# One row of u spread by a matrix product, the diagonal's fills in halves, and a planner with new durations

## The chip, the cores and the metric

The kernel runs on one core of a Trainium2 chip. The metric is the device time of one execution in microseconds. Five engines work side by side, each through its own instructions in order: TensorE (PE, with its weight loads, PEld, shown apart), VectorE (DVE), ScalarE (ACT), GpSimd (POOL) and SyncE (SP), which here only issues transfers.

## The reference, cut to what matters

A linear attention over 768 positions, 4 batches and 8 heads of width 48, whose output goes, token by token, through a feed-forward layer with a cosine gate:

```python
for t in range(S):                       # (B, H, S, D) = (4, 8, 768, 48)
    cur = einsum('bhd,bhe->bhde', u[None] * k[:, :, t], v[:, :, t])
    y[:, :, t] = einsum('bhd,bhde->bhe', r[:, :, t], state + cur)
    state = w[None, :, :, None] * state + einsum('bhd,bhe->bhde', k[:, :, t], v[:, :, t])
x = y.transpose(0, 2, 1, 3).reshape(3072, 384)
h = x @ w_in                             # (3072, 2048)
out = (h * cos(h)) @ w_out               # (3072, 384)
```

u, of shape (8, 48), weighs only the current position, so it enters on the diagonal of the position by position matrix alone.

## The kernel before, in words

The 3072 tokens are 24 chunks of 128 positions (chunk i is batch i % 4, position block i // 4). The function `chunk` does the attention of one chunk, and these are its steps with their lines in the kernel before:

- SP loads k, r and v of the chunk, 192 KB each, in pieces of 192 bytes (L638 for k and v, L654 for r). There are three buffers for k, three for v and two for r. From chunk 12 on, k and r are loaded a second time in another layout (L659), and r itself goes into one of the eight buffers `f`.
- PE transposes r and k (L696); DVE or ACT takes the result out of PSUM, with the decay factors (L721, L747, L756). From chunk 12 on DVE transposes instead (L704), and POOL applies the decay (L709).
- POOL multiplies r by k (L731), the product by u (L760), and k by its decay `dec_k` (L739). DVE sums L760's result by head (L766, `a`).
- ACT fills the diagonal: for each pair of heads it writes the identity times `a` into a 128x128 block of `A` (L775, eight instructions for each chunk, in two planned operations of four).
- PE computes the position by position products (L785); DVE copies their upper part over the diagonal (L791, needs the fills); PE makes x from the state (L805) and from `A` and v (L818), and the next state (L840). ACT and DVE split x into two parts (L868, L873).

The feed-forward layer runs over blocks of three chunks. A step is one slice f of 128 of the 2048 hidden columns: nine matmuls make h (L282), then ACT (`qi`, L293), DVE (`rest`, L296), ACT (`cos`, L299), DVE (`gate`, L986), ACT (`gh`, L989) and DVE (`gl`, L992) make the gated value in two parts, and nine matmuls (L288) add it to three accumulators. There are 128 such steps. Finished accumulators are copied out by ACT or DVE (L1019, L1021) and stored by SP, or added to the output in memory by POOL (L1034). Weights come as 64-bit numbers, 384 KB a piece (`raw`, L472 and L477, two buffers), and are converted by ACT, DVE and POOL (L556, L564, L576, L587, L592, L597). The buffers `f` are shared by the gates, by the products of L731, by conversion and by outputs.

The order of all this is not written out. Every piece of work is an `op` with an engine, a due time, a planned duration (`cost`), a planned latency (`lat`) until others may use its result, the ops it comes after, and its buffers. A list scheduler (`Plan.order`, L149) places the ops on the engines by these numbers, in five passes and one more, and picks buffers as it goes; the program is emitted in the planned order. Ops that share `line="..."` keep their order among themselves. While the first steps run, PE is kept busy by small matmuls on a tile of zeros ("warm-ups", L1050): one for each 0.2 us for which the plan sees PE idle (L1056 to L1059). So a changed duration anywhere can change the order everywhere.

Before the first chunk, w is loaded (L396), transposed (L401), raised to powers on DVE (L406 to L416) and spread to the decay tables `decT_k` and `decT_r` (L422); `dec_k` is `decT_k` transposed by PE (L438) and copied by ACT (L442). u is loaded by one transfer which reads the same 1536 bytes for each of the 128 partitions (L451).

Of the kernel before, what the change touches and what calls it, by code (L numbers as in the profile page):

```python
# [216 lines left out]
def kernel(  # L217
# [11 lines left out]
    nc = tc.nc  # L229
# [72 lines left out]
    with ExitStack() as actx:  # L302
# [80 lines left out]
        def start_dve():  # L383
            nc.vector.memset(warm, 0.0)
            nc.vector.memset(pq[:, :, 0:1], 1.0)

# [10 lines left out]
            [],  # L397
            lat=2.2,
        )
        b_w = Buf(B_EARLY)  # L400
# [30 lines left out]


        b_tab = Buf(B_EARLY)

# [5 lines left out]
        def tab_copy():  # L440
# [3 lines left out]
        o_tt = op(PE, -6, 0.5, tab_t, [o_dtk, o_pool], [b_tab], lat=0.3)  # L444
        o_dk = op(ACT, -6, 0.45, tab_copy, [o_tt], [b_tab])

        o_u = op(
            SP,
            -23.9,
            1.2,  # L450
            lambda: nc.sync.dma_start(u_b.rearrange("p h d -> p (h d)"), u.rearrange("h d -> (h d)").partition_broadcast(P)),  # L451
            lat=3.0,
        )

# [75 lines left out]
        def conv(i, due, behind=None):  # L530
# [17 lines left out]
            def cn():  # L548
# [13 lines left out]
                due - 2.1,  # L562
                0.33,
                lambda: nc.vector.tensor_scalar(  # L564
# [57 lines left out]
        def chunk(i, due, xbuf):  # L622
# [62 lines left out]
            if late:  # L685
                l_ks = op(SP, due - 6.2, 2.2, load_s(ks, k), ahead, [ks], lat=4.0, line=ln)
                l_rs = op(SP, due - 6.1, 2.2, load_s(rs, r), ahead, [rs], lat=4.0, line=ln)
            l_k = op(SP, due - 5.2, 1.2, load(kb, k), ahead, [kb], lat=2.6, line=ln)
            l_r = op(SP, due - 5.1, 1.2, load_r, ahead, [rb], lat=2.6, line=ln)
# [25 lines left out]
            else:  # L715
                t_r = op(PE, due - 2.4, 0.43, tr(rTp, rb), [l_r, o_pool], [rb, rTp, rT], lat=0.3)
                e_r = op(
# [23 lines left out]
            if first:  # L741
                t_k = op(PE, due - 2.5, 0.43, tr(kTp, kb), [l_k, o_pool], [kb, kTp, kT], lat=0.3)
                e_k = op(
                    DVE,
                    due - 2.3,
                    0.62,
                    lambda: nc.vector.tensor_tensor(kT()[0:KP], cube(kTp)[0:KP], decT_k[0:KP], op=ALU.mult),  # L747
                    [t_k, o_dtk],
                    [kTp, kT],
                )  # L750
                o_kd = op(e2, due + 1.0, c2, decay_k, [t_k, o_m, o_dk], [kb], port=True)
            else:
                o_kd = op(e2, due - 2.7, c2, decay_k, [o_m, o_dk], [kb], port=True)
            if not first and not late:
                t_k = op(PE, due - 2.5, 0.43, tr(kTp, kb), [o_kd, o_pool], [kb, kTp, kT], lat=0.3)
                e_k = op(ACT, due - 2.3, 0.5, lambda: nc.scalar.copy(kT()[0:KP], cube(kTp)[0:KP]), [t_k], [kTp, kT])  # L756
# [13 lines left out]

            def diagonal(j):
                def go():
                    for p in range(NP):
                        h = 2 * p + j
# [3 lines left out]

            o_d = [op(ACT, due - 1.55 + 0.01 * j, 1.18, diagonal(j), [o_a, o_pool], [ab, A[j]], line="diagonal") for j in range(2)]

# [5 lines left out]

            last_A[0] = o_A = op(PE, due - 1.7, 1.3 if late else 1.1, mm_a, [e_k, e_r], [kT, rT, *Ap], lat=0.3)

# [5 lines left out]

            e_A = [op(DVE, due - 1.4 + 0.01 * j, 0.65, mask(j), [o_A, o_d[j], o_pool2], [Ap[j], A[j]]) for j in range(2)]

# [54 lines left out]
            if late:  # L851
# [3 lines left out]
                    due - 0.7,  # L855
                    (0.9 if c else 0.0) + 1.3 + (0.55 if more else 0.0),
                    mm_xz,
# [4 lines left out]
            else:  # L862
                xo1 = None
                if c:
                    xo1 = op(PE, due - 0.7, 0.8, mm_x, [e_r, *e_A, *o_zt], [rT, xp, zb], lat=0.3)
                xo2 = op(PE, due - 0.65, 1.03, mm_x2, [xo1, l_v, o_pool, *e_A], [vb, *A, xp], lat=0.3)

# [334 lines left out]
```

## Time and profile before

| what | us |
|---|---|
| median of 3 runs (lowest, highest) | 518.86 (518.16, 519.00) |
| the profiled execution's own time | 519.36 |
| its span, first to last instruction | 517.6 |
| busy: PE, DVE, ACT, POOL | 505.2, 392.2, 331.7, 176.7 |
| mean granted TensorE clock, share of full speed | 0.995 |

Times in the profile are microseconds from the span's start. "Busy" of PE counts a matmul until its modelled end, so it can show 10 of 10 us although matmuls overlap; an idle gap of PE is a real gap. Warm-ups count as busy. In a row of the waits, "A <- B" says that A sat idle until B ended. The chain of waits follows the work that ended last back to the start.

### The profile page before, as it was taken

How to read it: one execution, taken by the hardware profiler on the slowest of the kernel's cores; microseconds unless marked ns; L12 is line 12 of the kernel's file. 1: busy time of each engine (PE TensorE's matmuls, PEld its weight loads, DVE VectorE, ACT ScalarE, POOL GpSimd, SP SyncE). 2: the span in 40 equal slices, each digit the busy share in tenths (PEclk: the TensorE clock that was granted, in tenths of full speed). 3: DMA queues.
4: the chain of work that ended last, by engine and by line, in shares of the span. 5: the costliest groups of instructions: out<-in, count | busy, mean ns of one | idle time of the engine just before them, and what ended most of it. 6: DMA issues, size and time to landing. Idle time of an engine off the chain costs nothing.

```text
span 517.6 us, 11730 instructions
## 1 busy us (share of the span) xinstructions
PE 505.2 (98%) x4401; PEld 480.6 (93%) x4401; DVE 392.2 (76%) x773; ACT 331.7 (64%) x833; POOL 176.7 (34%) x184
## 2 busy tenths in 40 slices
PE   8999999999999999999999999999999999999994
PEld 5788889999999998999999999999999999999993
DVE  6789988888888887666777887788787767766552
ACT  3889987777677765536566566585665765654452
POOL 6786522354454434232425134134134041300000
PEclk9999999999999999999999999999999999999998
DMA  8988345468556475424585646456536555210001
GB/s 133 174 159 188 72 139 182 146 134 180 137 139 131 114 164 97 78 61 69 144 152 120 150 129 169 89 177 155 132 85 154 170 136 121 80 46 2 2 0 53
DMA packets 114980, 61.61 MB, mean 119 GB/s; under 512 B 78433, under 2 KB 110818, under 8 KB 114914
## 3 DMA queue, kind: packets, MB, share of 16 engines
q1 hardware_dynamic: 109586, 53.50, 41.6%
q0 software_dynamic: 5184, 7.08, 9.2%
q8 instruction: 36, 0.59, 0.5%
q14 instruction: 30, 0.25, 0.2%
q10 hardware_dynamic: 144, 0.20, 0.1%
HBM read 48.96 MB, written 11.80 MB: 117 GB/s over the span
## 4 chain that ended last, share of the span: by engine, by line
PE 90%; DMA 3%; DVE 2%; POOL 1%; ACT 0%; issue 0%; SPq 0%; DVEq 0%; POOLq 0%; ACTq 0%
PE bank L288 38%; PE bank L282 37%; PE bank L785 4%; PE bank L818 4%; PE bank L805 3%; PE bank L696 2%; PE bank L840 2%; DMA raw<-in_moe_w_in_dram 1%; DMA r<-in_r_dram 1%; DMA u_b<-in_u_dram 1%; DVE gl L992 1%; DVE f L296 0%; POOL f L587 0%; POOL k L739 0%; POOL f L760 0%
## 5 line engine op out<-in xcount | busy, mean ns | idle before, releaser
L288 PE MATMUL bank<-w_out_hi,gh 128*128 128x384 f32 x384 | 131.4, 342 | 0.1
L288 PE MATMUL bank<-w_out_hi,gl 128*128 128x384 f32 x384 | 129.8, 338 | 1.3 <-DVE gl L992 1.3
L282 PE MATMUL bank<-xh,w_in_hi 128*128 128x384 f32 x384 | 130.1, 339 | 0.0
L282 PE MATMUL bank<-xh,w_in_lo 128*128 128x384 f32 x384 | 129.5, 337 | 0.0
L288 PE MATMUL bank<-w_out_lo,gh 128*128 128x384 f32 x384 | 129.5, 337 | 0.0
L282 PE MATMUL bank<-xl,w_in_hi 128*128 128x384 f32 x384 | 128.8, 335 | 0.0
L992 DVE TENSOR_TENSOR gl<-f,gh 128x384 fp32r<-128x384 f32 (+1 forms) x132 | 84.4, 642 | 28.2 <-ACT gh L989 27.2
L299 ACT ACTIVATE f<-f 128x384 f32<-128x384 f32 (+1 forms) x132 | 67.3, 513 | 52.7 <-DVE f L296 50.8
L293 ACT ACTIVATE qi<-bank 128x384 int32<-128x384 f32 (+1 forms) x132 | 62.7, 478 | 59.1 <-PE bank L282 58.1
L986 DVE TENSOR_TENSOR f<-bank,f 128x384 f32<-128x384 f32 (+1 forms) x132 | 71.2, 542 | 35.6 <-ACT f L299 32.9
L296 DVE SCALAR_TENSOR_TENSOR f<-bank,qi 128x384 f32<-128x384 f32 (+1 forms) x132 | 71.0, 541 | 34.8 <-ACT qi L293 33.9
L989 ACT CAST gh<-f 128x384 fp32r<-128x384 f32 (+1 forms) x132 | 65.8, 500 | 47.0 <-DVE f L986 41.7
L288 PEld LDWEIGHTS bank<-w_out_hi,gh 128*128 128x128 f32 x384 | 72.0, 187 | 2.7 <-ACT f L1019 0.5
L282 PEld LDWEIGHTS bank<-xh,w_in_hi 128*128 128x128 f32 x384 | 72.1, 188 | 1.7 <-issue 0.2
L288 PEld LDWEIGHTS bank<-w_out_hi,gl 128*128 128x128 f32 x384 | 72.0, 188 | 1.6 <-DVE gl L992 1.6
L282 PEld LDWEIGHTS bank<-xh,w_in_lo 128*128 128x128 f32 x384 | 72.1, 188 | 0.2 <-DVE w_in_lo L597 0.2
L282 PEld LDWEIGHTS bank<-xl,w_in_hi 128*128 128x128 f32 x384 | 72.1, 188 | 0.0
L288 PEld LDWEIGHTS bank<-w_out_lo,gh 128*128 128x128 f32 x384 | 72.0, 187 | 0.0
L775 ACT ACTIVATE A<-ident,a 128x128 f32<-128x128 f32 x192 | 59.9, 390 | 2.3 <-DVE a L766 2.3
L587 POOL TENSOR_TENSOR f<-f,raw 128x384 int32<-128x384 int32 x32 | 36.1, 1129 | 72.5 <-DVE f L576 19.4
L709 POOL TENSOR_TENSOR kT<-kT,decT_k 112x512 f32<-112x512 f32 x12 | 16.4, 1365 | 125.8 <-DVE kT L704 87.4
L1034 POOL DMA_DIRECT2D out_dram<-f x36 | 33.1, 1144 | 32.0 <-ACT f L1019 27.9
(88 smaller groups left out, 601.9 us busy)
## 6 DMA issues: line engine op xcount, KB each, us to landing
raw<-in_moe_w_in_dram SPq DMA_DIRECT2D x32, 384.0 KB, 3.8
raw<-in_moe_w_out_dram SPq DMA_DIRECT2D x32, 384.0 KB, 3.1
out_dram<-f POOLq DMA_DIRECT2D x36, 192.0 KB, 5.3
k<-in_k_dram SPq DMA_DIRECT2D x24, 192.0 KB, 4.1
v<-in_v_dram SPq DMA_DIRECT2D x24, 192.0 KB, 4.7
raw<-in_k_dram SPq DMA_DIRECT2D x47, 96.0 KB, 3.1
raw<-in_r_dram SPq DMA_DIRECT2D x47, 96.0 KB, 2.1
out_dram<-f SPq DMA_DIRECT2D x23, 192.0 KB, 2.3
```

Of the source, the lines that this page charges most:

```text
L282: nc.tensor.matmul(ph, a, b_, start=(i == 0), stop=(i == len(mm) - 1))
L288: nc.tensor.matmul(acc, a[:, ts], b_[:, f, :], start=(first and i == 0), stop=(last and i == 2))
L293: nc.scalar.activation(qi, ph, AF.Copy, scale=INV_2PI, bias=0.25)
L296: nc.vector.scalar_tensor_tensor(q, ph, INV_2PI, qi, op0=ALU.mult, op1=ALU.subtract)
L299: nc.scalar.activation(q, q, AF.Sin, scale=TWO_PI, bias=0.5 * math.pi)
L587: lambda: nc.gpsimd.tensor_tensor(ai(), ai(), cn(), op=ALU.add),
L775: nc.scalar.activation(A[j]()[:, p, :], ident, AF.Copy, scale=ab()[:, h : h + 1])
L785: nc.tensor.matmul(cube(Ap[j])[:, p, :], kT()[ps, p, :], rT()[ps, p, :], start=True, stop=True)
L986: nc.vector.tensor_tensor(g()[:, cs], ph()[:, cs], q()[:, cs], op=ALU.mult)
L989: nc.scalar.copy(gh()[:, cs], g()[:, cs])
L992: nc.vector.tensor_tensor(gl()[:, cs], g()[:, cs], f32(gh())[:, cs], op=ALU.subtract)
L1034: nc.gpsimd.dma_start(dst, ob(), accum_op=ALU.add)
```

## The change

There are four edits.

1. u is loaded as one row of 1536 bytes into partition 0 of its table. PE multiplies a row of 128 ones (kept in the first row of `dec_k` until that is written) by it, which gives u in all 128 partitions in PSUM, and ACT copies it to the table. The write of `dec_k` now also comes after that product.
2. The diagonal's fills, planned as two operations of four instructions (1.18 each), are four operations of two (0.59 each). The instructions are the same.
3. Planned durations are altered: 0.33 to 0.27 for a DVE step of the conversion, 0.43 to 0.49 for PE's transposes, 1.3 to 1.25 for the late chunks' products, 1.03 to 1.06 for x, and the late chunks' combined x and state by 0.25 at most.
4. The load of w and the load of k of the first chunk are put on one line, so they keep their order.

```diff
+            nc.vector.memset(dec_k.rearrange("p h d -> p (h d)")[0:1, 0:P], 1.0)
...
+        u_f, ones = u_b.rearrange("p h d -> p (h d)"), dec_k.rearrange("p h d -> p (h d)")[0:1, 0:P]
+        b_u = Buf(B_EARLY)
+        o_u0 = op(SP, -23.9, 0.1, lambda: nc.sync.dma_start(u_f[0:1], u.rearrange("(o h) d -> o (h d)", o=1)), lat=2.2)
+        o_u1 = op(
+            PE,
+            -20,
+            0.6,
+            lambda: nc.tensor.matmul(b_u()[:, 0:DM], ones, u_f[0:1], start=True, stop=True),
+            [o_u0, o_dve],
+            [b_u],
+            lat=0.3,
+        )
+        o_u = op(ACT, -20, 0.45, lambda: nc.scalar.copy(u_f, b_u()[:, 0:DM]), [o_u1], [b_u])
...
-        o_dk = op(ACT, -6, 0.45, tab_copy, [o_tt], [b_tab])
-
-        o_u = op(
-            SP,
-            -23.9,
-            1.2,
-            lambda: nc.sync.dma_start(u_b.rearrange("p h d -> p (h d)"), u.rearrange("h d -> (h d)").partition_broadcast(P)),
-            lat=3.0,
-        )
+        o_dk = op(ACT, -6, 0.45, tab_copy, [o_tt, o_u1], [b_tab])
...
-                0.33,
+                0.27,
...
-                t_r = op(PE, due - 2.4, 0.43, tr(rTp, rb), [l_r, o_pool], [rb, rTp, rT], lat=0.3)
+                t_r = op(PE, due - 2.4, 0.49, tr(rTp, rb), [l_r, o_pool], [rb, rTp, rT], lat=0.3)
...
-            def diagonal(j):
+            def diagonal(j, ps):
                 def go():
-                    for p in range(NP):
+                    for p in ps:
...
-            o_d = [op(ACT, due - 1.55 + 0.01 * j, 1.18, diagonal(j), [o_a, o_pool], [ab, A[j]], line="diagonal") for j in range(2)]
+            o_d = [
+                [
+                    op(ACT, due - 1.55 + 0.01 * j, 0.59, diagonal(j, ps), [o_a, o_pool], [ab, A[j]], line="diagonal")
+                    for ps in ((0, 1), (2, 3))
+                ]
+                for j in range(2)
+            ]
```

The whole order comes out anew. Three places show it; lines of the kernel after are higher by 1 to 15 (L647 and L663 are the loads of k, v and of r, L481 a piece of w_in, L718 the decay on POOL, L740, L748 and L769 the products by k, `dec_k` and u, L1049 the output's accumulating store). A name's number is its buffer.

The first place is the start of SP's queue, where the loads of w, u and the first chunks stand. Before:

```order
L396 DMA wr<-in_w_dram 4x2x48
L638 DMA k_86<-in_k_dram 128x8x48
L654 DMA r_84<-in_r_dram 128x8x48
L451 DMA u_b<-in_u_dram 128x384
L638 DMA k_87<-in_k_dram 128x8x48
L654 DMA r_85<-in_r_dram 128x8x48
L638 DMA v_89<-in_v_dram 128x8x48
```

After, the same stretch:

```order
L397 DMA wr<-in_w_dram 4x2x48
L437 DMA u_b<-in_u_dram 1x384
L647 DMA k_86<-in_k_dram 128x8x48
L663 DMA r_84<-in_r_dram 128x8x48
L647 DMA v_89<-in_v_dram 128x8x48
L647 DMA k_87<-in_k_dram 128x8x48
L663 DMA r_85<-in_r_dram 128x8x48
```

u has moved ahead of the first k and is one row; v of chunk 0 has moved ahead of k and r of chunk 1.

The second place is SP's queue from r of chunk 2 (the second use of buffer 84) to r of chunk 4 (its third). Before:

```order
L654 DMA r_84<-in_r_dram 128x8x48
L638 DMA v_90<-in_v_dram 128x8x48
L654 DMA r_85<-in_r_dram 128x8x48
L638 DMA k_86<-in_k_dram 128x8x48
L638 DMA v_91<-in_v_dram 128x8x48
L654 DMA r_84<-in_r_dram 128x8x48
```

After:

```order
L663 DMA r_84<-in_r_dram 128x8x48
L647 DMA v_91<-in_v_dram 128x8x48
L663 DMA r_85<-in_r_dram 128x8x48
L647 DMA k_86<-in_k_dram 128x8x48
L481 DMA raw_118<-in_moe_w_in_dram 128x3x256
L647 DMA v_89<-in_v_dram 128x8x48
L647 DMA k_87<-in_k_dram 128x8x48
L663 DMA r_84<-in_r_dram 128x8x48
```

As many loads stand ahead of r of chunk 3 (buffer 85) as before; but between it and r of chunk 4 there are now four transfers, one of them the first piece of w_in, where there were two. On PE, which then transposes r of chunk 4, the plan has put four warm-ups in front of those transposes; before there were none.

The third place is POOL's queue around chunk 12, the first one that POOL itself decays. Before:

```order
L709 TENSOR_TENSOR kT_94<-kT_94,decT_k 112x512
L1034 DMA out_dram<-f_112 128x384
L1034 DMA out_dram<-f_108 128x384
L1034 DMA out_dram<-f_110 128x384
L731 TENSOR_TENSOR f_111<-f_106,k_86 128x384
L709 TENSOR_TENSOR rT_96<-rT_96,decT_r 112x512
L760 TENSOR_TENSOR f_111<-f_111,u_b 128x384
L739 TENSOR_TENSOR k_86<-k_86,dec_k 128x8x48
```

After:

```order
L718 TENSOR_TENSOR kT_94<-kT_94,decT_k 112x512
L740 TENSOR_TENSOR f_108<-f_106,k_86 128x384
L718 TENSOR_TENSOR rT_96<-rT_96,decT_r 112x512
L748 TENSOR_TENSOR k_86<-k_86,dec_k 128x8x48
L769 TENSOR_TENSOR f_108<-f_108,u_b 128x384
L1049 DMA out_dram<-f_105 128x384
L1049 DMA out_dram<-f_107 128x384
L1049 DMA out_dram<-f_106 128x384
```

The three stores of a finished block stood ahead of the chunk's four products and now stand behind them, and the product by u has become the last of the four.

More of the change, by code (lines that the diff above doesn't have):

```diff
@@ L398 @@
             lat=2.2,
+            line="begin",
         )
@@ L687, in chunk @@
                 l_rs = op(SP, due - 6.1, 2.2, load_s(rs, r), ahead, [rs], lat=4.0, line=ln)
-            l_k = op(SP, due - 5.2, 1.2, load(kb, k), ahead, [kb], lat=2.6, line=ln)
+            l_k = op(SP, due - 5.2, 1.2, load(kb, k), ahead, [kb], lat=2.6, line="begin" if i == 0 else ln)
             l_r = op(SP, due - 5.1, 1.2, load_r, ahead, [rb], lat=2.6, line=ln)
@@ L741, in chunk @@
             if first:
-                t_k = op(PE, due - 2.5, 0.43, tr(kTp, kb), [l_k, o_pool], [kb, kTp, kT], lat=0.3)
+                t_k = op(PE, due - 2.5, 0.49, tr(kTp, kb), [l_k, o_pool], [kb, kTp, kT], lat=0.3)
                 e_k = op(
@@ L754, in chunk @@
             if not first and not late:
-                t_k = op(PE, due - 2.5, 0.43, tr(kTp, kb), [o_kd, o_pool], [kb, kTp, kT], lat=0.3)
+                t_k = op(PE, due - 2.5, 0.49, tr(kTp, kb), [o_kd, o_pool], [kb, kTp, kT], lat=0.3)
                 e_k = op(ACT, due - 2.3, 0.5, lambda: nc.scalar.copy(kT()[0:KP], cube(kTp)[0:KP]), [t_k], [kTp, kT])
@@ L785, in mm_a @@
                         nc.tensor.matmul(cube(Ap[j])[:, p, :], kT()[ps, p, :], rT()[ps, p, :], start=True, stop=True)
-            last_A[0] = o_A = op(PE, due - 1.7, 1.3 if late else 1.1, mm_a, [e_k, e_r], [kT, rT, *Ap], lat=0.3)
+            last_A[0] = o_A = op(PE, due - 1.7, 1.25 if late else 1.1, mm_a, [e_k, e_r], [kT, rT, *Ap], lat=0.3)
             def mask(j):
@@ L793, in mask @@
                 )
-            e_A = [op(DVE, due - 1.4 + 0.01 * j, 0.65, mask(j), [o_A, o_d[j], o_pool2], [Ap[j], A[j]]) for j in range(2)]
+            e_A = [op(DVE, due - 1.4 + 0.01 * j, 0.65, mask(j), [o_A, *o_d[j], o_pool2], [Ap[j], A[j]]) for j in range(2)]
             def xv():
@@ L855, in chunk @@
                     due - 0.7,
-                    (0.9 if c else 0.0) + 1.3 + (0.55 if more else 0.0),
+                    (0.8 if c else 0.0) + 1.15 + (0.5 if more else 0.0),
                     mm_xz,
@@ L865, in chunk @@
                     xo1 = op(PE, due - 0.7, 0.8, mm_x, [e_r, *e_A, *o_zt], [rT, xp, zb], lat=0.3)
-                xo2 = op(PE, due - 0.65, 1.03, mm_x2, [xo1, l_v, o_pool, *e_A], [vb, *A, xp], lat=0.3)
+                xo2 = op(PE, due - 0.65, 1.06, mm_x2, [xo1, l_v, o_pool, *e_A], [vb, *A, xp], lat=0.3)
             x_h = op(ACT, due - 0.4, 0.42, lambda: nc.scalar.copy(xbuf()[0], xv()), [xo2], [xp, xbuf])
```

## The prediction

> **What bounds the kernel now.** I read the page's first lines, then the busy time by stretch, then PE's waits, then the chain of waits over the first 72 us.
>
> ```profile
> span 517.6 us, 11730 instructions
> PE 505.2 (98%) x4401; PEld 480.6 (93%) x4401; DVE 392.2 (76%) x773; ACT 331.7 (64%) x833; POOL 176.7 (34%) x184
> ```
>
> ```profile
> 0.00:10.00 10.00, 7.70 (x48) 5.22 (x48) 6.00 (x21) 1.96 (x3) 5.79 (x21) 1.00 0.70 122
> 10.00:20.00 10.00, 8.93 (x154) 7.11 (x153) 7.66 (x14) 7.55 (x24) 8.15 (x9) 1.00 1.21 164
> 20.00:30.00 10.00, 10.00 (x187) 8.21 (x184) 8.06 (x16) 9.39 (x30) 7.45 (x8) 1.00 0.93 175
> 30.00:40.00 10.00, 9.89 (x186) 8.23 (x184) 9.19 (x18) 8.41 (x25) 8.55 (x9) 1.00 0.92 176
> ...
> 150.00:200.00 50.00, 48.75 (x279) 48.43 (x278) 41.69 (x75) 31.51 (x69) 23.41 (x23) 1.00 0.70 147
> 200.00:250.00 50.00, 50.00 (x422) 48.24 (x422) 32.30 (x62) 29.26 (x71) 11.19 (x11) 1.00 0.37 72
> ...
> 500.00:518.00 18.00, 10.07 (x58) 9.75 (x56) 6.03 (x22) 6.08 (x22) 0.00 (x0) 0.86 0.11 39
> ```
>
> The columns after the stretch and its length are the busy time of PE, PEld, DVE, ACT and POOL, then clock, DMA share and GB/s. PE sets the time: after the first 20 us it is idle for 0.11 us in one early stretch, for 1.25 us between 150 and 200, and for 7.93 us at the tail after its last matmul. The clock is full. The matmuls are the same in both kernels but for one, so the change can only move PE's idle time and its warm-ups. Where that idle time comes from is in PE's waits (total us, times, longest):
>
> ```profile
> PE bank L288 <- DVE gl L992: 1.3, 1, 1.3
> PE bank L1050 <- DVE pq L385: 1.1, 1, 1.1
> PE bank L696 <- DMA r<-in_r_dram: 1.1, 2, 0.8
> PE bank L438 <- DVE decT_k L422: 0.7, 1, 0.7
> PE bank L696 <- DMA k<-in_k_dram: 0.5, 2, 0.3
> ```
>
> Four of the five belong to the start; the first is the gap near 197. The chain shows which wait of the start ends last (start, us, what):
>
> ```profile
> 2.83 5.29 DMA u_b<-in_u_dram
> ...
> 8.25 1.31 POOL f L760
> ...
> 10.50 1.01 POOL f L731
> ...
> 11.53 5.47 DMA r<-in_r_dram
> ...
> 17.04 0.65 PE bank L696 x4
> 17.70 0.11 PE bank L1050
> ...
> 20.21 1.09 PE bank L785 x16
> ...
> 21.88 0.49 PE bank L840 x16
> 22.38 0.58 PE bank L696 x4
> ```
>
> u lands at 8.12, POOL's three products follow, the third frees r's buffer for chunk 3, that load lands at 17.00, and PE, which had only warm-ups until then, goes on and has hardly a gap after it. At 22.38 it transposes r of chunk 4 without a wait.
>
> **Part 1: u as one row.** What the old transfer cost its neighbours is seen in three landings on which somebody waited:
>
> ```profile
> 6.07 1.01 POOL L731 TENSOR_TENSOR f<-r,k 128x384 f32<-128x384 f32 x1 [2.27 <-DMA r<-in_r_dram]
> ```
>
> ```profile
> 10.33 0.62 PE L696 MATMUL bank<-ident,r 128*112 128x128 f32 x4 [0.27 <-DMA r<-in_r_dram]
> ...
> 13.85 0.40 PEld L696 LDWEIGHTS bank<-ident,r 128*112 128x112 f32 x4 [0.20 <-DMA r<-in_r_dram]
> ```
>
> r of chunk 0, 1 and 2 are there by 6.07, 10.33 and 13.85. Between the last two lie three ordinary loads (v0, k2, r2): 3.52 us, 1.17 each. Between the first two lie u, k1 and r1: 4.26 us. So u took 4.26 - 2 x 1.17 = 1.92 us of the transfer queue, 0.75 more than an ordinary load. The new row adds an issue ahead of everything; the nearest row is the load of w as one row of the same length near the end:
>
> ```profile
> L459 SPq DMA_DIRECT2D f<-in_w_dram x1: 308/308/308, 463.9 to 463.9; - x1
> ```
>
> That is 0.31 us. An ordinary load stands where u stood, so from r1 on everything in the same place of the queue lands 0.75 - 0.31 = 0.44 us earlier, and r of chunk 3 at 17.00 - 0.44 = 16.56. It can't be held up by its issue: POOL's L731 of chunk 1, at 10.50 before, still waits for r1 (10.33 - 0.44) and for `dec_k`, and two loads are queued between r1's landing and r3's. The product by ones stands behind w's transpose on PE and needs a row issued right behind w's, before the first k has landed; ACT is idle then. I cost both at nothing; bounds 0 to 0.4 (the row late by one issue), hidden by the wait for k.
>
> With u there early, POOL's L760 follows L731 without the gap from 7.08 to 8.25. In that gap DVE made the decay tables; an op of DVE that met POOL's L731 there was held:
>
> ```profile
> 6.23 0.86 DVE L406 TENSOR_TENSOR cq<-pq 128x4 f32<-128x4 f32 x1
> ```
>
> A second POOL product at once could hold the tables for 1.0 us more. PE would then come to r of chunk 3 about 0.5 us after it has landed, at 17.1, as late as now. What follows is set by r of chunk 4, so I cost this at 0.
>
> **Part 2: the new queue up to r of chunk 4.** After r3 now come k3, a piece of w_in, v3, k4 and r4. Four ordinary loads are 4.68 us. The piece has no row of its own in a full queue; it has twice the bytes of an ordinary load,
>
> ```profile
> raw<-in_moe_w_in_dram SPq DMA_DIRECT2D x32, 384.0 KB, 3.8
> ...
> k<-in_k_dram SPq DMA_DIRECT2D x24, 192.0 KB, 4.1
> ```
>
> so it takes between one and two slots, 1.17 to 2.34 (by time to landing the two are alike, which speaks against the upper end; I take the middle, 1.75). r4 lands at 16.56 + 4.68 + 1.75 = 23.0 (22.4 to 23.6). PE arrives there at 22.37 - 0.44, and four warm-ups of 0.11 later it is 22.37. It waits 0.6 us, and what stood at 22.38 stands at 23.0: **+0.6 us (0.0 to +1.2)**. PE's own start gains nothing from u any more; the wait for r3 has become one for r4. Behind it in PE's queue are the products of chunk 3 and all that follows, nothing of which can go ahead.
>
> Later in the start there is little to win back: 0.11 us idle, and these warm-ups (busy, count):
>
> ```profile
> 20.00:30.00 10.00, 0.39 (x2) 0.11 (x2) 1.00 0.93 175
> 30.00:40.00 10.00, 0.28 (x1) 0.10 (x1) 1.00 0.92 176
> ```
>
> Three at 0.11 make 0.33. The plan after has two left there. I take **-0.2 (-0.4 to 0)**.
>
> **Part 3: halves and durations.** The fills are the same instructions, so their cost is nothing in itself; they and the durations act through the order alone. The one place after 40 us where PE loses time that an order can give back is the gap at 197. The rows of DVE and of POOL there:
>
> ```profile
> 190.44 0.56 DVE L992 TENSOR_TENSOR gl<-f,gh 128x384 fp32r<-128x384 f32 x1 [0.66 <-ACT gh L989]
> ...
> 194.50 4.46 DVE L992 TENSOR_TENSOR gl<-f,gh 128x384 fp32r<-128x384 f32 x1
> ```
>
> ```profile
> 192.64 2.67 POOL L1034 DMA_DIRECT2D out_dram<-f  x3 [2.17 <-ACT f L1019]
> 194.36 2.00 POOL L731 TENSOR_TENSOR f<-f,k 128x384 f32<-128x384 f32 x1
> 195.34 2.25 POOL L709 TENSOR_TENSOR rT<-rT,decT_r 112x512 f32<-112x512 f32 x1
> 196.58 1.95 POOL L760 TENSOR_TENSOR f<-f,u_b 128x384 f32<-128x384 f32 x1
> 197.56 2.25 POOL L739 TENSOR_TENSOR k<-k,dec_k 128x384 f32<-128x384 f32 x1
> ```
>
> A `gl` that takes 0.56 us takes 4.46 while POOL runs four products in a row, which had gathered behind three stores; PE waits 1.3 us for it. In the new order the stores come behind the products, so each product can start when its own input is there, and I expect `gl` to get in between: **-1.3 us (-1.3 to 0)**. The Trainium skill ("SBUF — State Buffer", section "SBUF: two separate sides") says that DVE's second port is shared with GpSimd and held for one whole instruction. By that alone `gl` would wait for one product, about 1 us, and PE not at all; the trace has it wait for four, so the row decides, and the gap can come back wherever four gather. By the page the sum would be the same -1.3, only surer.
>
> Elsewhere PE has nothing to give back (0 idle from 200 to 250), so the rest of the new order can only lose; I take 0, bounds 0 to +2.
>
> The tail after the last matmul has the same ops in the same order: 0.
>
> **Sum.** +0.6 - 0.2 - 1.3 = -0.9 us. The profiled execution took 519.36 (span 517.6 and 1.8 around it), 0.5 above the median, so it would come to 518.5; on the median of 518.86 that is **518.0**. A measurement of this kernel can tell about 0.2%, 1.04 us, from no change.
>
> **The rivals.**
>
> *The start keeps its gain.* If the piece of w_in moves in gaps of the queue, r4 is there by 22.0 and the 0.44 survive: -0.44 - 0.4 - 1.3 = -2.1, 516.7. For it: the time to landing of a piece is no longer than that of a load. Against: the DMA share of 0.92 to 1.21 between 10 and 40 leaves few gaps.
>
> *The gap moves instead of going.* Four POOL products gather behind something else, a late load of chunk 12 for one, and hold a `gl` again: +0.6 - 0.2 = +0.4, 519.3. For it: all four still stand next to each other in POOL's queue.
>
> *Stores late, slower.* At chunk 12 the stores now wait behind the products. The four products took from 194.36 to 199.81, 5.45 us; if they start no sooner than before, three of the eight buffers `f` are held that much longer, and the gates of the next steps run out of buffers. PE has about one step in hand, nine matmuls for h and nine for o:
>
> ```profile
> 189.74 1.58 PE bank L282 x9
> ```
>
> 2 x 1.58 = 3.2. So it decides from a delay of 3.2 us on and costs 5.45 - 3.2 = 2.3 us: -0.9 + 2.3 = +1.4, 520.3. For it: r of the late chunk also sits in such a buffer. Against: the gates need about two of the eight at a time.
>
> **How the numbers follow.** The forecast, -0.9 with its own range of -1.5 to -0.3 (r4's bounds; 517.4 to 518.6), has 0.42; about 0.17 of this lies beyond -1.04. The start keeping its gain 0.21, the gap moving 0.17, late stores 0.20. Faster: 0.17 + 0.21 and 0.02 for the edges, 0.40. Same: 0.25 of the forecast less those edges and 0.14 of the moved gap, 0.37. Slower: 0.20 and 0.03, 0.23. The range, 516.4 to 520.2, reaches from just past the first rival to most of the last.
>
> **What would show it.** In PE's waits after: the row for gl at 1.3 gone, the wait for r still there but at about 22.4 instead of 16, up to 1.2 us long. POOL's L760 no longer waiting for u. r of chunk 3 landing near 16.6. Wrong if PE's idle time between 20 and 40 exceeds 1.3 us, if PE waits for a copy or a buffer at a block's border, or if a DVE row of over 4 us stands anywhere after 40 us with PE idle behind it.

## The result and the profile after

The changed kernel takes 523.21 us, median of 7 runs (520.72 to 523.84), against 519.0 us of the kernel before (7 runs, 518.16 to 519.86): 1.0064 times as long, with a 95% interval of 1.0045 to 1.0082. The forecast was 518.0 with a range up to 520.2, so the sign was wrong (-0.9 forecast, +4.2 measured) and the result lies outside the range. A second set of runs of the same kernel gave 522.44 (6 runs), ratio 1.0056 [1.0038, 1.0074].

The first lines of the page of the changed kernel; its profiled execution took 521.80:

```profile
span 520.0 us, 11740 instructions
PE 507.9 (98%) x4402; PEld 481.9 (93%) x4402; DVE 389.3 (75%) x774; ACT 331.0 (64%) x834; POOL 179.5 (35%) x184
```

Stretches of the changed kernel, some of them further than the prediction showed (columns: stretch, length, then busy us of PE, PEld, DVE, ACT, POOL):

```profile
20.00:30.00 10.00, 10.00 (x176) 8.37 (x172) 8.01 (x15) 9.02 (x29) 6.90 (x8) 1.00 1.16 188
30.00:40.00 10.00, 9.22 (x167) 7.48 (x165) 9.59 (x18) 7.87 (x24) 8.01 (x8) 1.00 0.87 170
40.00:50.00 10.00, 10.00 (x228) 8.10 (x231) 9.46 (x19) 9.90 (x32) 7.08 (x8) 1.00 0.71 158
50.00:60.00 10.00, 9.56 (x171) 7.43 (x162) 9.59 (x20) 9.62 (x29) 7.53 (x7) 1.00 0.61 143
60.00:80.00 20.00, 18.90 (x246) 16.55 (x247) 17.02 (x36) 16.08 (x42) 6.36 (x7) 1.00 0.34 110
150.00:200.00 50.00, 49.95 (x286) 49.62 (x285) 40.50 (x76) 32.91 (x75) 23.22 (x24) 1.00 0.62 133
```

The kernel before had no idle time of PE in three of them:

```profile
40.00:50.00 10.00, 10.00 (x216) 8.45 (x215) 9.17 (x19) 9.79 (x29) 5.92 (x6) 1.00 0.80 162
50.00:60.00 10.00, 10.00 (x200) 8.55 (x198) 9.70 (x18) 9.81 (x29) 7.44 (x7) 1.00 0.53 100
60.00:80.00 20.00, 20.00 (x232) 17.73 (x227) 17.94 (x41) 16.79 (x42) 4.31 (x4) 1.00 0.44 138
```

So the 1.25 us idle between 150 and 200 are gone but for 0.05, as forecast, and 0.78, 0.44 and 1.10 us stand between 30 and 80, where the kernel before had 0.11. PE's waits name them (total us, times, longest):

```profile
PE bank L705 <- POOL k L748: 1.4, 1, 1.4
PE bank L1065 <- DVE warm L384: 1.1, 1, 1.1
PE bank L282 <- DVE A L806: 0.8, 1, 0.8
PE bank L705 <- DMA r<-in_r_dram: 0.6, 1, 0.6
PE bank L288 <- DVE gl L1007: 0.3, 1, 0.3
PE bank L282 <- DVE w_in_lo L606: 0.2, 1, 0.2
```

The wait of 1.3 for `gl` at 198 is gone (the 0.3 stands at 139.7). New are three more: a transpose of k waits 1.4 for POOL's decay, the first h waits 0.8 until DVE's mask has read a PSUM bank that h takes over, and an h waits 0.2 for converted weights. The first is at 61; POOL, then DVE, then PE there:

```profile
57.15 1.01 POOL L740 TENSOR_TENSOR f<-r,k 128x384 f32<-128x384 f32 x1
58.24 2.81 POOL L748 TENSOR_TENSOR k<-k,dec_k 128x384 f32<-128x384 f32 x1
```

```profile
58.15 0.36 DVE L902 TENSOR_TENSOR zc<-zc,pq 112x192 f32<-112x192 f32 x1
58.42 0.35 DVE L573 TENSOR_SCALAR f<-raw 128x384 int32<-128x384 int32 x1
58.69 0.55 DVE L606 TENSOR_TENSOR w_in_lo<-f,w_in_hi 128x384 fp32r<-128x384 f32 x1
59.16 0.55 DVE L585 SCALAR_TENSOR_TENSOR f<-raw,f 128x384 int32<-128x384 int32 x1
59.63 0.55 DVE L1007 TENSOR_TENSOR gl<-f,gh 128x384 fp32r<-128x384 f32 x1
60.10 0.72 DVE L806 COPY_PREDICATED A<-upper,bank 128x512 f32<-128x512 int32 x1
```

```profile
61.10 0.65 PE L705 MATMUL bank<-ident,k 128*112 128x128 f32 x4 [1.38 <-POOL k L748]
```

The decay takes 1.02 us elsewhere and 2.81 here: it stands while DVE's steps on SBUF follow each other without a break, three of them weight conversions, and ends 1.0 us after DVE has come to a mask, which reads PSUM. I read it as the wait of `gl` beside POOL in the kernel before, the other way round; two experiments below bear on it.

To place the loss I use one number worked out from the traces, **PE's lag**: the time at which a group of matmuls starts, less what all groups ahead of it take when nothing holds them up (for each pair of successive kinds of group, the lower quartile of the start-to-start times in the trace of before). It grows where PE is held up.

| PE's lag, us | third chunk's products (20 us) | first h | fourth h (66 to 68 us) | 21st h (122 to 127 us) | chunk 12's products (219 to 222 us) | last h |
|---|---|---|---|---|---|---|
| before | 10.50 | 11.47 | 11.86 | 12.81 | 14.82 | 18.27 |
| after | 9.98 | 11.86 | 14.43 | 15.33 | 16.57 | 20.01 |
| after, second profile | 9.89 | 11.74 | 14.10 | 14.99 | 16.40 | 19.84 |

The start is 0.5 better; from there to the fourth h the changed kernel loses 4.45 against 1.36; then it wins 0.8 around 197. The last matmul ends at 512.39, before at 510.07: +2.3, of which the lag places +1.7. The lag rests on typical times of pairs of groups, and between two orders I take it as good to about 0.6 us, the part of the 2.3 that it does not place. The idle time alone points to the same place: between 34 and 80 PE is idle for 2.33 us in the changed kernel and for none in the kernel before.

### The profile page after: what moved, and what is told of

It reads as the page before. It is cut to its first block, busy times and chain, and to the rows that moved or that the text cites. A ratio compares the mean times of both kernels' runs of the same rounds, so it can differ in the third digit from the quotient of the medians.

```text
span 520.0 us, 11740 instructions
## 1 busy us (share of the span) xinstructions
PE 507.9 (98%) x4402; PEld 481.9 (93%) x4402; DVE 389.3 (75%) x774; ACT 331.0 (64%) x834; POOL 179.5 (35%) x184
## 4 chain that ended last, share of the span: by engine, by line
PE 84%; DVE 4%; DMA 3%; ACT 3%; POOL 2%; issue 2%; SPq 1%; POOLq 0%; ACTq 0%
PE bank L288 37%; PE bank L282 36%; PE bank L800 3%; PE bank L833 3%; PE bank L820 2%; ACT A L784 2%; DMA r<-in_r_dram 2%; DMA f<-in_r_dram 1%; PE bank L855 1%; DVE A L806 1%; POOL f L740 1%; PE bank L705 1%; DVE zc L902 1%; POOL k L748 1%; DVE a L775 1%
## 5 line engine op out<-in xcount | busy, mean ns | idle before, releaser
L1007 DVE TENSOR_TENSOR gl<-f,gh 128x384 fp32r<-128x384 f32 (+1 forms) x132 | 82.6, 630 | 30.2 <-ACT gh L1004 30.0
L718 POOL TENSOR_TENSOR kT<-kT,decT_k 112x512 f32<-112x512 f32 x12 | 15.8, 1316 | 126.2 <-DVE kT L713 95.5
L1049 POOL DMA_DIRECT2D out_dram<-f x36 | 32.1, 1122 | 35.0 <-ACT f L1034 32.5
```

Of the source, the lines that this page charges most:

```text
L718: return lambda: nc.gpsimd.tensor_tensor(dst()[0:KP], dst()[0:KP], dec[0:KP], op=ALU.mult)
L1007: nc.vector.tensor_tensor(gl()[:, cs], g()[:, cs], f32(gh())[:, cs], op=ALU.subtract)
L1049: nc.gpsimd.dma_start(dst, ob(), accum_op=ALU.add)
```

## The experiments

Two theories were put to the test first. Theory 1: the order that the planner draws from the new numbers loses, at single places of the attention stage, and u's row is harmless. Theory 2: u's row costs by itself. Further ones are named where they come up. The kernel before, measured again beside each of four groups of runs, took 519.18, 519.24, 519.24 and 519.64 us.

| run | median us (runs) | ratio to before, 95% | last matmul ends | from there to the span's end |
|---|---|---|---|---|
| before, after | 519.0, 523.21 (7, 7) | 1.0064 [1.0045, 1.0082] | 510.07, 512.39 | 7.5, 7.6 |
| before's order, u's row | 523.08 (6) | 1.0075 [1.0048, 1.0102] | 513.80 | 7.0 |
| after's order, old transfer | 523.28 (6) | 1.0078 [1.0053, 1.0103] | 513.71 | 7.3 |
| u's row alone | 518.99 (12) | 0.9989 [0.9975, 1.0004] | 509.68 | 8.3 |
| halves alone | 520.81 (12) | 1.0038 [1.0020, 1.0055] | 511.07 | 7.2 |
| durations alone | 519.54 (11) | 0.9992 [0.9981, 1.0004] | 508.93 | 8.4 |
| u's row and halves | 519.48 (12) | 0.9997 [0.9985, 1.0008] | 508.94 | 8.7 |
| u's row and durations | 518.36 (12) | 0.9983 [0.9971, 0.9994] | 510.30 | 5.8 |
| before's order, row first | 520.18 (12) | 1.0023 [1.0009, 1.0037] | 510.70 | 8.0 |
| after, decay first | 522.10 (6) | 1.0070 [1.0042, 1.0098] | 511.01 | 7.6 |
| row and durations, store moved | 518.50 (12) | 0.9981 [0.9971, 0.9992] | 510.49 | 5.5 |
| before, no branch | 514.44 (6) | 0.9915 [0.9900, 0.9930] | 508.83 | 3.5 |
| after, no branch | 518.46 (12) | 0.9989 [0.9977, 1.0000] | 513.16 | 3.4 |
| after, decay first, no branch | 517.59 (6) | 0.9952 [0.9937, 0.9968] | 513.94 | 3.4 |
| after, light pieces, no branch | 516.08 (6) | 0.9933 [0.9918, 0.9949] | 510.29 | 3.5 |
| before, light pieces, no branch | 516.10 (6) | 0.9932 [0.9916, 0.9948] | 510.93 | 3.5 |

**The order held, u exchanged.** In the first kernel only u's way differs from before, in the second only u's way differs from after.

```diff
 # before's order, u's row: on SP at the old transfer's place, behind k and r of chunk 0
-nc.sync.dma_start(u_b, u.partition_broadcast(P))
+nc.sync.dma_start(u_f[0:1], u as one row)
+nc.tensor.matmul(u_ps, ones, u_f[0:1])   # PE: right behind w's transpose
+nc.scalar.copy(u_f, u_ps)                # ACT: ahead of dec_k's copy
 # after's order, old transfer
-nc.sync.dma_start(u_f[0:1], u as one row)
+nc.sync.dma_start(u_f, u.partition_broadcast(P))
-nc.tensor.matmul(b_u, ones, u_f[0:1])
-nc.scalar.copy(u_f, b_u)
```

> The order of the kernel before on every engine, with u alone brought in as one row (its transfer in the old one's place, the product on PE right behind w's transpose, ACT's copy ahead of the copy of dec_k). Theory 1, the time is lost by the new order of the attention stage and u's row is harmless: r of chunk 3 lands about 0.7 us earlier (an ordinary load's slot instead of u's 1.9 us), the wait for it shrinks, and the kernel is within 1.0 us of the kernel before, rather 0.3 to 0.7 us faster. Theory 2, u's row itself costs (a product that holds PE's first transposes, a row that lands late, GpSimd's product by u running into VectorE's decay tables): slower by 2 us or more, the loss before 20 us in the trace.

> The order of the changed kernel on every engine, with u loaded to all partitions by one transfer as before (in the new row's place, ahead of the first k), without product and copy. Theory 1 (the order costs, not u's row): as slow as the changed kernel or a little slower, 523 to 525 us, since all loads of the start land up to 1.9 us later; PE still waits near 35, 55 and 59 us. Theory 2 (u's row costs): back to 519 to 520.5 us.

The second is as slow as the changed kernel and has its waits, the 1.4 for the decay among them; a wait of 2.0 for the first k, behind u's transfer, comes on top, and its last matmul is 1.3 later than the changed kernel's. So the loss does not need u's row. The first missed: 523.08, for a reason of my own making. The row came behind k and r of chunk 0, the product stood ahead of chunk 0's transposes, and PE waited at the head of its queue:

```profile
5.99 1.61 PE L408 MATMUL bank<-u_b,dec_k 1*128 1x384 f32 x2 [2.13 <-DMA u_b<-in_u_dram]
```

The lag was 10.08 at PE's first product of `A` and v against 8.18 before, and 21.50 at the last h. So 1.9 us were lost at the start and not made good; of the 3.7 us at the last matmul, most of the rest stands in one wait that the kernel before does not have, 1.7 us at 116 for ACT's copy of a finished accumulator. With the row put right behind w's load:

> The kernel before with its order on every engine, u as one row loaded right behind w's transfer and ahead of chunk 0's k, the product behind w's transpose, the copy ahead of the k table's copy; nothing else differs. The earlier try of this had the row behind chunk 0's k and r, and PE waited 2.1 us for it at the head of its queue. Theory 1 (the row is harmless, the new order loses): the product stands before 5 us with no wait over 0.6; r of chunk 1 lands 0.5 to 1.5 earlier than 10.3; lag at the first products of masks within 0.5 of 8.2; time 518.0 to 519.7. Theory 2 (the row costs by itself, by the product's place or the copy): lag there 9.2 or more, time 520.5 or more.

It took 520.18, 0.5 over what theory 1 allowed and 0.3 under theory 2. In its trace the product stands at 3.73 without a wait, r of chunk 1 has landed at 9.16, the lag at the first product of `A` and v is 8.42, and at the third chunk's products and the last h it is 10.35 and 18.40, within 0.2 of before. So by the lag u's row costs nothing, and by the times at most 0.5 to 1.9 us (the interval), far from 3 to 4. A gain is not there either: r of chunk 3 landed at 17.37, 0.37 later than before, because POOL waited for `dec_k` ahead of the product that frees its buffer. What the 0.9 of the medians is stays open.

**One edit alone, and two.** The planner orders each of these kernels anew.

```diff
 # u's row alone: edits 1 and 4; halves alone: edit 2; durations alone: edit 3
-o_d = [op(ACT, ..., 1.18, diagonal(j), ...) for j in range(2)]
+o_d = [[op(ACT, ..., 0.59, diagonal(j, ps), ...) for ps in ((0, 1), (2, 3))] for j in range(2)]
```

> The change's edits 1 and 4 alone (u as a row, w and the first k on one line); fills whole, durations as before. The planner makes an order of its own from it: the first piece of w_in stands in place 13 of SP's queue, ahead of k of chunk 3. Theory 1: what counts is how far the weights' conversion is drawn into the attention stage, where ScalarE and VectorE have little to spare; it is drawn forward here too, so PE waits between 30 and 70 us, and the kernel is 1 to 4 us slower than before. Rival: the halves or the durations make the loss; then this one is within 1 us of the kernel before or faster.

> The change's edit 2 alone: the diagonal's fills planned as four operations of two instructions; u and the durations as before. The first piece of w_in stays in place 18 of SP's queue, as in the kernel before, the second moves up by three places. Theory 1: the start is as before, so PE's waits before 70 us stay small, within 1 us of the kernel before. Rival (finer fills let the plan put other work between a chunk's fills, and each chunk's diagonal ends later on ScalarE): slower by 1 to 3 us, with PE waiting for masks (VectorE's copy over the diagonal).

> The kernel before with the planned durations alone; the planner orders it anew (its third to fifth weight pieces come after 24, 36 and 36 of the early loads). Theory 1 (no edit loses by itself, the order that the three draw together does): no PE wait over 0.6 us between 34 and 80 us, 518.0 to 520.5. Rival (the durations make the order that loses): 521.5 or more, with waits for POOL or for conversions at 34 to 62 us.

> The kernel before with u's row and product and with the fills in halves, the planned durations as they were; the planner orders it anew. Theory 1 (it is the order that the planner happens to draw that loses, not one edit): the weights' third to fifth pieces come after 24, 34 and 36 of the early loads (26, 28, 33 before; 23, 27, 32 in the changed kernel), so fewer conversions meet the attention stage: 518 to 521. Theory 2 (u's row costs by itself): 522 or more, as the row is in it. Theory 3 (the halves cost by themselves, since eight fills of ACT take the same time in four instructions' groups but let others in between): 520 to 521, as with the halves alone.

> The kernel before with u's row and product and the planned durations as traced, the fills whole. Theory 1: the order again is another (pieces after 22, 35, 36 of the early loads, later than in the changed kernel), no long wait of PE for POOL or for conversions between 34 and 80 us: 518 to 520.5. Theory 2: 522 or more. Theory 3 (the halves are what costs): below 519.5. If both this and the kernel with u's row and the halves stay under 521, no single edit makes the loss and only all three together draw the order that loses.

No edit comes near 523, and neither does either pair tried; halves with durations were not tried. Halves alone lose 1.6 us, 0.9 of it at the gap at 197, where PE's wait for `gl` is 2.2 in place of 1.3:

```profile
PE bank L288 <- DVE gl L998: 2.2, 1, 2.2
```

With u's row added that wait is gone, and the time is 519.48, under the 520 to 521 of theory 3 (the halves cost by themselves), which so falls. Durations alone have no wait of PE over 1.1 us, and none over 0.4 but the one for the warm-ups' zeros at the very start. So no edit has a price of its own that adds to the others': each set of numbers draws another order, and of those tried the order of all three together is the one that loses. Theory 2 falls.

One expectation missed in a way that matters. With u's row alone, early weight pieces were to make the kernel 1 to 4 us slower: its second to fifth piece are loaded after 17, 24, 30 and 36 of the chunks' 36 early loads, not far from the changed kernel's 17, 23, 27 and 32. It took 518.99, and PE has no idle time between 34 and 80. Nor has it with u's row and either other edit; with halves alone it has 0.17, with durations alone 0.26. So early pieces by themselves do not make the loss; what they meet in the attention stage does.

**The wait at 61.** One weight piece's addition on POOL goes behind chunk 11's product and decay, and its two next steps go back on ACT and DVE.

```diff
 # POOL
-f_109 + raw_119          # weight piece 4
 f_106 = r * k            # chunk 11
 k * dec_k                # chunk 11
+f_109 + raw_119
```

> The changed kernel with three instructions of one weight piece moved back: its addition on POOL goes from ahead of chunk 11's r-k product and k decay to behind them, its rounding on ACT behind the next qi, its remainder on DVE behind the second mask. Nothing is left out. Theory 1 (the new order loses at single places, the largest being PE's 1.4 us wait at 59 us for the k decay, which took 2.81 us in place of 1.02 because DVE's four weight and gate steps from 58.42 to 60.10 ran back to back): the decay ends before 57.8 with about 1.0 us, the wait goes, PE's lag at the steps of 68 us falls from 14.4 by 1.3 to 1.5, and the time falls by 1.0 to 1.5 from the changed kernel's 523.2, to 521.7 to 522.2. Theory 1b (the wait covers another that is as late, such as the rounding for ACT or the reload of the raw piece): the wait at 59 goes and another of 0.8 us or more stands before 80 us; the time stays within 0.5 of 523.2. Theory 2 (u's row costs by itself): within 0.5 of 523.2, lag lost elsewhere.

> The changed kernel itself once more, for a second profile: its profiled run (521.8) was 1.4 us shorter than the median of its timed runs (523.2), so a wait of some tenths to 1.5 us should stand in this profile that the first does not show. Theory 1: it stands where POOL and DVE meet in the attention stage or behind it (36 to 62 us, or 113 to 200 us), and its size differs between executions of one program. Theory 2: it stands at the start, before 16 us, around u's row and product. If the second profile is again near 521.8, nothing is told apart.

The decay now runs undisturbed, and the transpose behind it comes without a wait (POOL, then PE):

```profile
57.37 1.02 POOL L751 TENSOR_TENSOR k<-k,dec_k 128x384 f32<-128x384 f32 x1
58.34 1.42 POOL L598 TENSOR_TENSOR f<-f,raw 128x384 int32<-128x384 int32 x1
```

```profile
59.77 0.65 PE L708 MATMUL bank<-ident,k 128*112 128x128 f32 x4
```

The lag at the fourth h is 13.10, at the last h 18.63, 1.3 to 1.4 under after; the last matmul ends at 511.01. The times did not show it: 522.10, with one run of 526.13 among six, is within the spread of after, which took 522.44 beside it. PE's idle time between 34 and 80 fell from 2.33 to 0.74. The second profile of after has the same chief waits as the first (1.4 for the decay; 0.7 in place of 0.3 for `gl`), and its 520.6 us of span are 0.6 above the first, all of it behind the last matmul (512.22). So no wait of 1.5 us was hidden from the first profile.

**Without the branch at the end.** The kernel ends in a branch to code for values out of range, which is not entered here. With branch and code left out, the same inputs give the same work. The two expectations call it theory 3 that the jump over this code makes the rest of the difference.

```diff
-with tc.If(ok < 1):
-    ...
```

> The kernel before without the branch at its end: the code for weights or decays out of range, which these inputs never enter, is left out. PE's last product and its waits should stand where they did (510.1). Theory 3 (the engines' jump over that code costs a varying part of the 5.7 to 8.7 us between PE's last product and the end of the span, which differs from kernel to kernel with where the code lies): this stretch falls to 4.5 to 5.0 us and the time by 2 to 3.5, to about 516. If not, only the stores' landing sets it, and the time stays within 0.5 of 519.2.

> The changed kernel without that branch, same part left out. Its profile's last product stands 2.2 us after that of the kernel before (512.3 against 510.1), its median 3.4 to 4.2. Theory 3 (the rest of the difference, 1 to 2 us, is the jump at the end): without the branch the two kernels differ by 2.0 to 2.5. If the difference stays at 3.3 or more, the rest lies in waits that the two profiles of the changed kernel do not show in full, such as gl behind POOL at 135 to 200 us.

The stretch from PE's last matmul to the end fell to 3.4 to 3.5 in both, more than expected. But the two kernels still differ by 4.0 us, so this theory falls: the difference is PE's, 4.3 at the last matmul. The lag at the third chunk's products was 9.62 and 9.96, at the fourth h 10.81 and 14.60, at the last h 17.04 and 20.78. The loss stands where it stood. With less spread the decay could be tried again:

> The changed kernel with one weight piece's addition behind chunk 11's k decay, as tried before, and without the branch at the end (the code for values out of range, not entered here, is left out), since the runs without it spread less. Theory 1 (PE's wait for the decay at 59 us is worth what it shows): 1.0 to 1.5 under the changed kernel without the branch (518.46), so 517.0 to 517.5. Theory 1b (what is won there is lost again further on): within 0.4 of 518.46.

It took 517.59, just over the 517.0 to 517.5 of theory 1. The two kernels were not measured side by side: by medians it gains 0.9, by the ratios to before (0.9989 and 0.9952) 1.9. Its profiled execution, 519.41, was the slowest of its six, with other waits, so its trace settles nothing.

**The conversions made light.** Three of the six steps of the weight pieces 1 to 4 (counted from 0) work on 32 of 384 columns, in both kernels, in unchanged order; the other columns of these pieces are left unconverted.

```diff
+n = 32 if 1 <= i <= 4 else DM
-nc.gpsimd.tensor_tensor(ai(), ai(), cn(), op=ALU.add)
+nc.gpsimd.tensor_tensor(ai()[:, 0:n], ai()[:, 0:n], cn()[:, 0:n], op=ALU.add)
 # and so the step on ACT (low words) and one of DVE's (joining)
```

> The changed kernel without the branch at the end, and with three of the six steps of the weight pieces 1 to 4 (ACT's low words, DVE's joining, POOL's addition) on 32 of 384 columns, so that these pieces' values are left unfinished; every instruction stays in its place. Theory 1c (the rest of the loss is that these conversions stand inside the attention stage, where ACT and DVE have nothing to spare): the lag at the steps of 68 us falls by 1.5 or more from 14.6, the time to 515.5 to 517.0 from 518.46, and the difference to the kernel before treated alike falls from 4.0 to 2.5 or less. Rival (the conversions do not matter, the chain of fills and masks ahead of the first h and the banks do): 517.8 or more, the difference 3.5 or more.

> The kernel before, treated as the other: no branch, the same three steps of pieces 1 to 4 on 32 columns, which leaves them unfinished. Theory 1c: these conversions stand later there, where PE's own work covers them, so the time stays within 0.5 of 514.44. Rival: it gains as much as the changed kernel does.

516.08 and 516.10 are equal, but only one side of this is as expected. The changed kernel came down by 2.4, as theory 1c (the conversions inside the attention stage are the rest of the loss) had it. These two were not measured side by side with the kernels with full conversions; by the ratios to before the changed kernel came down by 2.9, and the kernel before went up by 0.9. Its first h no longer waits for the mask, and its longest wait behind the start's is this one, at 35; the 1.4 at 61 is gone with its cause:

```profile
PE bank L707 <- POOL k L750: 0.6, 1, 0.6
```

From the third chunk's products to the fourth h its lag grows by 2.28 (10.40 to 12.68), with full conversions by 4.64 (9.96 to 14.60), so they make 2.4 of the loss there; PE's idle time between 34 and 80 falls from 2.53 to 0.59. The kernel before missed its expectation: by medians it went up by 1.7, from 514.44. Its trace shows where:

```profile
PE bank L698 <- DMA r<-in_r_dram: 1.3, 1, 1.3
```

That is the load of r for chunk 3 at 16 us, ahead of all that was changed; without the branch alone it cost 0.3. From the third chunk's products to the fourth h it loses nothing more (10.62 to 11.81, 1.19 as without the change); a wait of 0.6 at 113 for ACT's copy of a finished accumulator comes later. Against the changed kernel's 2.28 that leaves 1.1 of the loss to the order's other places. Why this load lands up to 1 us apart in programs that are alike up to there was not found; it bounds what a comparison of two single kernels here can say to about 1 us.

**The gap at 198, a way to close it.** In the kernel with u's row and the durations one store goes between POOL's products.

```diff
 # POOL
-store out
 f_105 * u_b              # chunk 12
+store out
 rT * decT_r
```

> The kernel with u's row and the planned durations, with one instruction moved: on POOL one output store goes from ahead of chunk 12's product by u to right behind it, so that POOL's three products at 195.5 no longer follow each other without a break; nothing is left out. Theory 1 (at 195.7 DVE's gl waits for as long as POOL's multiplications follow one another, and gets in at the first break): gl takes under 1.8 us in place of 3.46, PE's wait of 1.3 us at 198 goes, the time falls by 1.0 to 1.3 to 517.0 to 517.4. Theory 1b (gl waits for all of POOL's products or for something else): gl over 3 us, the time stays within 0.4 of 518.4. Rival: POOL's later decay of r and k becomes what PE waits for at chunk 12's products of 220 us; then the gain is under 0.4.

A miss: `gl` takes 3.53 us in place of 3.46. DVE, then POOL:

```profile
195.82 3.53 DVE L1004 TENSOR_TENSOR gl<-f,gh 128x384 fp32r<-128x384 f32 x1
```

```profile
195.10 1.64 POOL L772 TENSOR_TENSOR f<-f,u_b 128x384 f32<-128x384 f32 x1
196.07 1.51 POOL L1046 DMA_DIRECT2D out_dram<-f  x1
196.69 2.20 POOL L721 TENSOR_TENSOR rT<-rT,decT_r 112x512 f32<-112x512 f32 x1
197.94 2.25 POOL L751 TENSOR_TENSOR k<-k,dec_k 128x384 f32<-128x384 f32 x1
```

A store between two products is no break that lets DVE in. `gl` ends 0.46 after the product behind the store, at 199.35, and 0.84 ahead of the end of the last one (200.19), which follows without a break. The version stays at 0.9981 [0.9971, 0.9992], and it and its parent are the fastest of those that keep the branch. They owe it to the end: their last matmul is 0.2 to 0.4 later than before's, the stretch behind it 1.7 to 2.0 shorter.

## Why the prediction was wrong, step by step

**The step that failed** is in part 3, the sentence ahead of the tail: "Elsewhere PE has nothing to give back (0 idle from 200 to 250), so the rest of the new order can only lose; I take 0, bounds 0 to +2." The direction of this term was right and its size was not. Its bounds of 0 to +2 were not carried into the sum's own range of -1.5 to -0.3 either, and no rival gave them a price. The lag shows +0.5 from r of chunk 4 to the first h (0.92 before, 1.38 after) and +2.2 from there to the fourth h: +2.7, where I had 0 for this term and -0.2 for the warm-ups of the later start. I had counted moved steps by their own cost, which is nothing, and had looked for waits that the new order could free. I did not ask which steps it brings together. The rows to ask were there: between 30 and 60 (two of them stand above) DVE and ACT of before are busy 8.4 to 9.8 of 10 us. In that stage the planner now loads the second to fifth weight piece after 17, 23, 27 and 32 of the chunks' 36 early loads, where the kernel before does so after 26, 28, 33 and 36 (the expectation for u's row and halves gives 26, 28 and 33 as its third to fifth; they are the second to fourth). What the experiments show in its place: light conversions take 2.4 of the 4.0 away, in the stage where the lag said it was lost; part of that is the wait of 1.4 at 61, POOL's decay beside three conversion steps and a `gl`, which one piece moved back removes. That pieces come early is not enough, as u's row alone shows; by the lag about 1.1 of the loss there belongs to other places of this order, which were not tried one by one.

**Part 1, u as one row.** PE's share was right: the product ran at 3.73, hidden. The step "It can't be held up by its issue" failed. r of chunk 3 was issued at 12.60 instead of 11.53 and landed at 16.99, as late as before (17.00) and not at 16.56. The chain of waits has it (start, us), and POOL's rows show why:

```profile
12.60 4.39 DMA r<-in_r_dram
```

```profile
6.64 1.56 POOL L740 TENSOR_TENSOR f<-r,k 128x384 f32<-128x384 f32 x1 [2.85 <-DMA r<-in_r_dram]
8.27 1.33 POOL L769 TENSOR_TENSOR f<-f,u_b 128x384 f32<-128x384 f32 x1
10.59 1.02 POOL L748 TENSOR_TENSOR k<-k,dec_k 128x384 f32<-128x384 f32 x1 [0.98 <-ACT dec_k L459]
11.56 1.01 POOL L740 TENSOR_TENSOR f<-r,k 128x384 f32<-128x384 f32 x1
```

r of chunk 0 is there 0.6 later than before (behind the row's issue), its product is held for half a microsecond beside DVE's tables, and the product by u starts at 8.27, where before it started at 8.25 after waiting for u. The k decay then waits for `dec_k`, the product of chunk 1 that frees r's buffer runs 1.06 later, and the load with it. That the tables would come up to 1.0 later was in the text; that they stand ahead of the buffer was not followed. It cost nothing in the sum, since PE came to r3 as late as forecast (17.03). The kernel before with the row first shows the same chain.

**Part 2.** The wait for r of chunk 4 did not come. It landed at 22.36 (forecast 22.4 to 23.6), ahead of PE, which transposed it at 22.73 with a lag 0.1 under that of before. The weight piece took 1.31 us of the queue, from k3 at 17.56 to 18.87, where I had put the middle, 1.75; the four loads took 4.06 in place of 4.68, k3 alone 0.57; and r3 was 0.43 late. The low end of the range was right, and the term +0.6 was -0.1. The first rival asked for r4 by 22.0; at 22.36 PE lost nothing to it all the same, but that gain was used up ahead of the first h.

**Part 3, the gap at 197.** Right in size: PE's wait of 1.3 for `gl` went, and the delay there, start to start, fell from 1.52 to 0.32. Its reason holds in half. DVE, then POOL:

```profile
190.73 3.60 DVE L1007 TENSOR_TENSOR gl<-f,gh 128x384 fp32r<-128x384 f32 x2
```

```profile
190.34 1.02 POOL L740 TENSOR_TENSOR f<-f,k 128x384 f32<-128x384 f32 x1 [4.50 <-ACT f L299]
191.32 1.61 POOL L718 TENSOR_TENSOR rT<-rT,decT_r 112x512 f32<-112x512 f32 x1
192.90 1.02 POOL L748 TENSOR_TENSOR k<-k,dec_k 128x384 f32<-128x384 f32 x1
193.88 1.32 POOL L769 TENSOR_TENSOR f<-f,u_b 128x384 f32<-128x384 f32 x1
```

The products did not spread: all four still follow each other without a break. But the first `gl` ended 0.42 after the first product, at 191.78, and the second, of 2.63 us, ended 0.41 after the third, at 194.33, ahead of the fourth, which took 1.32 where such a product takes 1.01 at 54.40. So each got in between, the second after two products, and PE had enough ahead to cover it. The prediction's row of before is to be read the same way: its `gl` ended at 198.96, 0.43 after the third product and 0.85 ahead of the end of the fourth, so it waited for three and not for four. A new wait for a `gl` beside POOL's addition, 0.3 at 139.7, took 0.56 of the gain back, and 0.94 in the second profile. The Trainium skill ("SBUF — State Buffer", section "SBUF: two separate sides") has the holder of the shared port keep it for one whole instruction. If that port is what they wait for, these rows, and the decay of 2.81 us beside four steps of DVE, show that it can pass to the same engine's next instruction while the other engine waits; they do not show what decides when it changes hands.

**The rivals.** None of the three came. The late stores did no harm, and the four products gathered again without holding PE. Of the signs named beforehand, two came: the row of 1.3 for `gl` went, and POOL's product by u no longer waits for u. PE's idle time between 20 and 40, 0.78, stayed under the 1.3 that was to prove it wrong; the nearest to a sign of being wrong is PE waiting 0.8 us for a PSUM bank at the first h, which is at no block's border. r of chunk 3 landed at 16.99 and not near 16.6, and the wait for r stayed at 17. No sign looked at 50 to 80, where most was lost. The tail, taken as 0, was 0.1 in the first profile and 0.9 in the second.

**What stays open.** The profiles of after are 2.4 and 3.0 us of span above that of before, the medians 3.2 to 4.2 us apart. Of PE's +2.3 the lag places 1.7. Halves with durations were not tried.

## What to carry to other kernels

When an order comes from a planner, new numbers are a new order, and its price is not the sum of the edits': check in the busy time by stretch where the engines beside the bound have nothing to spare, and see in the new order what has been moved into that stretch. A price of zero for a moved step holds only where its new neighbours have room. Before crediting a gain at the start, follow the freed transfer to the buffer that its successor needs, and to the engine that frees that buffer.

## What the runs showed of the hardware that was not expected

The hold between DVE and POOL works both ways and over several instructions: `gl` of 0.56 us took 4.46 beside POOL's products, a product of 1.02 took 2.81 beside DVE's steps. It does not last until the other engine pauses: a `gl` of 4.46, of 2.63 and of 3.53 us each ended 0.4 to 0.5 us after one product and ahead of the end of the next, which followed without a break. A store issued by POOL between its products did not shorten it (3.53 against 3.46).

The branch to code that is not entered cost 4.0 to 4.9 us at the end in the three kernels measured both ways: from the last matmul to the end of the span pass 7.5 to 8.4 us with branch and code and 3.4 to 3.5 without. Over all kernels with it the stretch is 5.5 to 8.7 us. It so differs from program to program more than the effect of some edits, so the end of the last matmul is the better measure of an order than the time. What sets it was not tried, and branch and code were only left out together.
